# The first pair's turned keys in a PSUM tile per quarter, and idle products beside the first head's first scores

## The chip, the cores and the metric

The kernel runs on one core of one Trainium2 chip. The metric is the device time of one execution in microseconds (us), as the median of several runs. Engines are named as in the profile: PE is the matrix engine (TensorE) and PEld its weight loads, DVE is VectorE, ACT is ScalarE, POOL is GpSimd, SP is SyncE, which issues transfers; an engine's name with a q is its sequencer, which also issues transfers on ACT.

## The reference

An attention block with a threshold is followed by a feed-forward block with an ELU. Cut to what matters:

```python
# attention: q, k, v are (8, 8, 576, 64), float32; tau is a scalar
scores = scale * q @ k.T                        # scale = 1/8
thresh = max(scores, -1) - tau
scores = where(scores >= thresh, scores, -1e9)
attn = exp(scores - max(scores, -1))
out  = (attn / (sum(attn, -1) + 1e-9)) @ v      # to (4608, 512), heads side by side
# feed-forward: w_in (512, 2048), w_out (2048, 512)
h = x @ w_in
g = where(h > 0, h, exp(min(h, 0)) - 1)
result = g @ w_out
```

## The kernel before

Attention works on pairs of heads: 4 pairs in each of 8 sequences. A pair's two heads of 64 dimensions lie in the upper and the lower half of the 128 partitions, head 0 in rows 0 to 63 and head 1 in rows 64 to 127, so that a score product has 64 rows of the array. A step takes 128 query rows (the last, of 64 rows, serves both heads at once) against all 576 keys, in two halves of 288 (`HALF`); 512 of the 576 positions are `MAIN`, 64 are `TAIL`. A score product in float32 is two PE records in the trace. Feed-forward work of earlier sequences is laid among the attention steps later on. The order of all instructions is written out ahead: tasks have due times, corrected by a table (`MOVED`), are sorted, and each engine runs its own in that order, with semaphores between the engines. The first task is `start`; the scores of step 0 come after it.

For most pairs VectorE turns queries and keys in 32 by 32 squares. The first pair is turned by PE, in `start`:

- Transfers. SP's queue takes head 0's keys (`kb[:, 0]`, 128 KB), head 1's keys (`kb[:, 1]`), `tau`, and the second block of queries; ACT's queue takes the first block of queries (`qb[:, 0]`) and the last 64 keys of both heads (`ends`).
- Five PSUM tiles: `blank` and `turned` from the pool `t` (two buffers of one bank), `a`, `b`, `c` from the pool `s` (three buffers of two banks). `c` is taken and not used. The scores of step 0 get the buffers of `a` (head 0) and `b` (head 1).
- PE multiplies ones by ones twice (L1364), runs 8 transposes of the identity into `blank` (`warm`, whose records stand under L800), turns the queries (L1357), then two blocks of keys of head 0 into `a` and two of head 1 into `b`, runs one more idle transpose, and turns `ends`. A turn is one record with all 128 rows; `ends` uses 64.
- Copies out of PSUM into one SBUF tile that holds `qT` and `kT` (it shows as `x`): VectorE copies the queries (L1367); of each head's keys VectorE and ScalarE copy one half each, 64 rows by 256 columns (L1374), both out of the same tile; VectorE copies `ends` to their two places (L1377, and L1378 for head 1).
- `read_tau` then has five small GpSimd steps (L440 to L444) on tau, whose results the thresholds need.

`scores` (L665) issues the products of a step at L681. For the first two steps (`HEADS_APART`) both halves of head 0 stand ahead of both halves of head 1. Right after step 0's scores PE turns the second block of queries, and ScalarE copies it (`rest_of_first_q`, L1383); in ScalarE's order that copy stands ahead of all work on step 0's scores. For each head of step 0 VectorE then takes the maximum (`max_of`, L738) and a threshold (`pivot_of`, L756), ScalarE makes two passes (`sink_of`, L761, and `raise_of`, L767), VectorE adds up and inverts, and GpSimd scales (`normalize`, L734).

Of the kernel before, what the change touches and what calls it, by code (L numbers as in the profile page):

```python
# [368 lines left out]
def kernel(  # L369
# [10 lines left out]
    nc = tc.nc  # L380
    PSUM = bass.MemoryType.PSUM
    P = 128
    B, H, S, D = q.shape
    DM, DF = moe_w_in.shape
    NC = S // P
    MAIN = NC * P
    TAIL = S - MAIN
# [40 lines left out]
    ident = wstage.tile([P, P], FP32, name="ident", bufs=1)  # L428
# [10 lines left out]
    def read_tau():  # L439
        nc.gpsimd.tensor_scalar(keep, tau_sb, 0.0, SCALE, ALU.is_ge, ALU.mult)  # L440
        nc.gpsimd.tensor_scalar(far, keep, -FAR / SCALE, FAR, ALU.mult, ALU.add)
        nc.gpsimd.tensor_scalar(floor, tau_sb, far, 1.0, ALU.max, ALU.mult)
        nc.gpsimd.tensor_scalar(ntau, floor, DEEP, -1.0, ALU.min, ALU.mult)
        nc.gpsimd.tensor_scalar(ntau0, floor, -1.0 / SCALE, 1.0, ALU.mult, ALU.mult)  # L444
# [119 lines left out]
    def room_q(pr):  # L564
        if pr < 2:
            both = wstage.tile([P, 2 * S + TAIL], FP32, name="x", bufs=2)
            qT, firsts[pr] = both[:, :S], both[:, S:]
        else:
            qT = qkp.tile([P, S], FP32, name="qT")
        pairs[pr] = [qT, None, qds[pr % NQD]]  # L570
        return qT

    def room_k(pr):
        kT = pairs[pr][1] = firsts[pr] if pr < 2 else qkp.tile([P, TAIL + S], FP32, name="kT")
        return kT
# [19 lines left out]
    def long_rows(name, i):  # L595
        return {"k": k, "v": v}[name][0, i, :MAIN].rearrange("(p c) d -> p c d", c=NC)

    def first_rows(name, c, n=P):
        return {"q": q, "k": k}[name][0, :2, c * P : c * P + n].rearrange("i p d -> p i d")
# [56 lines left out]
    def vectors(pr):  # L656
        st = {x: small.tile([P, 2], FP32, name=x) for x in ("mx", "th", "su", "rs")}
        if not pr:
            st["nb"] = wstage.tile([P, 2], FP32, name="nb", bufs=4)
        step_no[0] += 1  # L660
        st["sm"] = totals[:, step_no[0] % 6]
        return st


    def scores(pr, i, hs):  # L665
        qT, kT, qd = pairs[pr]
        if hs[0] == 0:
            open_steps[pr, i] = vectors(pr)
        st = open_steps[pr, i]
        if "f" in psum and not apart:  # L670
            both = psum["s"].tile([P, 2, 2, 512], FP32, name="sc")
            scs = {h: both[:, h] for h in hs}
        else:
            scs = {h: psum["s"].tile([P, 2, 512], FP32, name="sc") for h in hs}
        halves = [(a, h) for a in range(2) for h in hs]
        if (pr, i) in HEADS_APART:
            halves.sort(key=lambda x: x[1])
        for a, h in halves:
            k0 = a * HALF + (0 if h else TAIL)
            r, qs = (slice(h * D, (h + 1) * D), qT[:, i * P : (i + 1) * P]) if i < NC else (slice(0, P), qd)  # L680
            nc.tensor.matmul(scs[h][:, a, :HALF], qs[r], kT[r, k0 : k0 + HALF], start=True, stop=True)  # L681
        if len(hs) == 2 and "f" in psum and not apart:
            st["both"] = both
        for h in hs:
            st[h] = scs[h]
# [113 lines left out]
    def transpose(dst, src):  # L799
        nc.tensor.matmul(dst, src, idents[-1], is_transpose=True, skip_group_check=True)  # L800
# [390 lines left out]
    def heads_of(i):  # L1191
        return [0, 1] if i < NC else [0]
# [123 lines left out]
    def early_tasks():  # L1316
# [18 lines left out]
        def start():  # L1335
            tiles = raws[0] = {"km": raw.tile([P, S // T, T], FP32, name="km")}
            kb = tiles["km"].rearrange("p j d -> p (j d)")[:, :MAIN].rearrange("p (i e f) -> p i e f", i=2, e=2)
            qb = wstage.tile([P, 2, 2, D], FP32, name="qb", bufs=1)
            ends = tiles["ends"] = wstage.tile([TAIL, 2, D], FP32, name="ends", bufs=1)

            nc.sync.dma_start(kb[:, 0], long_rows("k", 0).rearrange("p (e o) d -> p e (o d)", o=2))
            nc.scalar.dma_start(qb[:, 0], first_rows("q", 0))
            nc.sync.dma_start(kb[:, 1], long_rows("k", 1).rearrange("p (e o) d -> p e (o d)", o=2))
            nc.scalar.dma_start(ends, first_rows("k", NC, TAIL))
            nc.sync.dma_start(tau_sb, tau.to_broadcast([P, 1]))
            nc.sync.dma_start(qb[:, 1], first_rows("q", 1))
            nc.scalar.activation(keep, keep, AF.Exp)
            blank, turned = (psum["t"].tile([P, NC, P], FP32, name="rt", tag="rt") for _ in range(2))
            a, b, c = (psum["s"].tile([P, 2, 512], FP32, name="sc") for _ in range(3))
            qT, kT = room_q(0), room_k(0)  # L1350

            def warm(n):
                for _ in range(n):
                    transpose(blank[:, 0], ident)

            def turn_rows(dst, src, n=P):
                nc.tensor.matmul(dst, src, ident[:n, :n], is_transpose=True, skip_group_check=True)  # L1357

            def flat(src):
                return src.rearrange("p i d -> p (i d)")  # L1360

            ones = nc.const_aps.tensor(1.0, [P, P])
            for x in range(2):
                nc.tensor.matmul(blank[:, x], ones, ones, start=True, stop=True)  # L1364
            warm(8)
            turn_rows(turned[:, 0], flat(qb[:, 0]))
            nc.vector.tensor_copy(qT[:, :P], turned[:, 0])  # L1367
            main = kT[:, TAIL:S].rearrange("p (e o n) -> p o e n", e=2, o=2)
            for h, room in ((0, a), (1, b)):
                r = slice(h * D, (h + 1) * D)  # L1370
                for e in range(2):
                    turn_rows(room[:, 0, e * P : (e + 1) * P], kb[:, h, e])
                for o, copy in ((h, nc.vector.tensor_copy), (1 - h, nc.scalar.copy)):
                    copy(main[r, o], room[o * D : (o + 1) * D, 0, : 2 * P].rearrange("p (e n) -> p e n", e=2))  # L1374
            warm(1)
            turn_rows(turned[:, 1, :TAIL], flat(ends), TAIL)
            nc.vector.tensor_copy(kT[:, S:], turned[:, 1, :TAIL])  # L1377
            nc.vector.tensor_copy(kT[D:, :TAIL], turned[D:, 1, :TAIL])  # L1378

            def rest_of_first_q():  # L1380
                rt = psum["t"].tile([P, NC, P], FP32, name="rt", tag="rt")
                turn_rows(rt[:, 0], flat(qb[:, 1]))
                nc.scalar.copy(qT[:, P : 2 * P], rt[:, 0])  # L1383

            first_q.append(rest_of_first_q)
            read_tau()

# [16 lines left out]
        def switch():  # L1404
            first.close()
            apart.append(True)
            for name, bufs in (("s", 2), ("f", 2)):
                psum[name] = banks.enter_context(tc.tile_pool(name=f"ps_{name}", bufs=bufs, space=PSUM))

        task("start", -100.0, None, start)  # L1410
        for x in ("q", "k"):
            made["prep", x, 0] = made["copy", x, 0] = made["start"]
# [10 lines left out]
        for pr in range(1, NPAIR + 6):  # L1423
            old = ("sc", number[pr - 2, NC]) if pr > 1 else None
            own = pr < NPAIR
            for x, name in enumerate("qk"):
                n = 2 * pr - 2 + x if own else number[pr - 1, 2 + x]
                k, late_ = kind(n), n >= LATE
# [30 lines left out]
            for x, name in enumerate("qk"):  # L1459
                n = 2 * pr - 1 + x if own else number[pr - 1, 3 + x]  # L1460
# [3 lines left out]
            if pr > 1:  # L1464
                n = 2 * pr - 3 if own else number[pr - 1, 3]
# [5 lines left out]
        for i, (n, x) in enumerate(slots):  # L1471
            late_, k, t = n >= LATE, f"{kind(n)}{x}", begin[n]
# [42 lines left out]
        rooms, exps, owner = [], [], {}  # L1515
        for u in range(NU):
            n = 26 + 3 * u // 2 if u < NU - 2 else SWITCH + u - NU + 2
# [3 lines left out]
        for n in range(MIDDLE):  # L1521
            pr, i = steps[n]
# [4 lines left out]
            t, k, hs, late_ = begin[n], kind(n), heads_of(i), n >= LATE  # L1527
# [3 lines left out]
            if n == LATE:  # L1531
                task("switch", t, None, switch, *rooms)
            rooms += [("exp" if (n, h) in MASK_ACT else "mask", n, h) for h in hs]
            at_ = (lambda a, b, c=0: t + c) if last_ else (lambda a, b, c=0: t + b) if late_ else (lambda a, b, c=0: t + a)
            task(("sc", n), t + 0.2 if late_ else t - 2.6 if i in (2, NC) else t - 2.0, f"sc{k}", lambda pr=pr, i=i, hs=hs: (scores(pr, i, hs), first_q and first_q.pop()()), ("prep", "q", pr),
                 ("prep", "k", pr), ("scale", pr) if pr else None, ("copy", "k", pr), ("copy", "q", pr) if i == NC else None,
                 ("sc", n - 1) if n else None, "rest" if (pr, i) == (0, 2) else None, *two)
# [128 lines left out]
    with tc.manual_schedule():  # L1666
# [31 lines left out]
        ends = []  # L1698
# [439 lines left out]
        for pr in range(JOINED, NP + 2):  # L2138
            t = clock[0]
            b = pr // NPAIR  # L2140
# [265 lines left out]
```

## Time and profile before

| | us |
|---|---|
| median of three timed runs | 1256.07 |
| lowest and highest of them | 1256.03, 1256.32 |
| the profiled execution | 1257.65 |
| its span, first to last instruction | 1255.8 |
| PE busy in the span | 1244.7 (99%) |
| DVE, POOL, ACT busy | 1040.4, 727.8, 636.2 |

In the prediction a row of the timeline is: start, length (us from the span's start), engine, line of the kernel, operation, output<-input by the program's names, shape, xcount, and in brackets the idle time before it with what ended it. Rows that follow each other on one engine are merged and counted, and a short slice shows only what was under way in it. A row of the chain of waits is start, length and what; a row of transfers ends with its size and the time from issue to landing. The busy tenths on the page are 40 slices of 31.4 us each.

### The profile page before, as it was taken

The page shows a single profiled execution, that of the slowest core. Times are in us where ns is not written, and L with a number is a line of the kernel's source. Part 1 is how long each engine was busy: PE and PEld are TensorE (multiplying, and loading weights), DVE is VectorE, ACT ScalarE, POOL GpSimd, SP SyncE. Part 2 cuts the span into 40 slices and gives each one's busy share as a digit, 9 for nine tenths or more (in the row PEclk, how much of TensorE's full clock was granted, in tenths as well). Part 3 has the DMA queues.
Part 4 walks back from the last instruction along what each step waited for, and adds up shares of the span by engine and source line. Part 5 has one row for each costly group of instructions (what it writes and reads, how often), then busy time and mean ns, then how long its engine had stood idle before and what let it go on. Part 6 is the DMA issues. An engine that isn't in the chain of part 4 may idle for free.

```text
span 1255.8 us, 21112 instructions
## 1 busy us (share of the span) xinstructions
PE 1244.7 (99%) x6596; PEld 956.9 (76%) x6596; DVE 1040.4 (83%) x2196; ACT 636.2 (51%) x1334; POOL 727.8 (58%) x1064
## 2 busy tenths in 40 slices
PE   8999999999999999999999999999999999999998
PEld 6675576477887787878778787878788887788887
DVE  7888777789798978998889889898889876776983
ACT  7899776664453526253534445352625353465330
POOL 5778655687575748676576747584767655122000
PEclk9999999999999999999999999999999999999999
DMA  7456788998889998898989997999889885000001
GB/s 149 146 171 184 172 244 235 257 269 217 228 240 255 247 246 233 225 259 226 263 206 253 235 232 230 259 251 244 229 228 268 221 242 174 20 1 1 1 34 34
DMA packets 322303, 245.74 MB, mean 196 GB/s; under 512 B 205456, under 2 KB 286736, under 8 KB 322192
## 3 DMA queue, kind: packets, MB, share of 16 engines
q1 hardware_dynamic: 321376, 243.78, 72.3%
q8 instruction: 52, 0.85, 0.3%
q10 hardware_dynamic: 816, 0.62, 0.2%
q14 instruction: 59, 0.48, 0.2%
HBM read 154.53 MB, written 89.78 MB: 195 GB/s over the span
## 4 chain that ended last, share of the span: by engine, by line
PE 91%; DVE 3%; DMA 2%; ACT 2%; issue 1%; SPq 1%; POOL 1%; DVEq 0%; ACTq 0%; POOLq 0%
PE f L1869 23%; PE f L1729 21%; PE sc L985 8%; PE sc L1058 7%; PE f L2332 7%; PE f L2257 5%; PE f L1110 4%; PE sc L681 3%; PE f L1162 3%; PE f L2270 2%; PE pv L938 2%; PE rt L800 2%; PE sc L1050 1%; DMA there<-x 1%; PE sc L1045 1%
## 5 line engine op out<-in xcount | busy, mean ns | idle before, releaser
L992 DVE TENSOR_REDUCE mx<-sc 128x1 f32<-128x576 f32 x207 | 148.3, 750 | 30.0 <-PE sc L985 26.1
L734 POOL TENSOR_SCALAR w<-w,rs 128x576 f32<-128x576 f32 x144 | 115.8, 813 | 69.6 <-DVE rs L797 69.5
L1012 ACT ACTIVATE w<-sc,mx 128x576 f32<-128x576 f32 x113 | 81.5, 740 | 115.6 <-DVE mx L992 98.7
L876 DVE STREAM_TRANSPOSE x<-w 128x512 f32<-128x512 f32 (+1 forms) x153 | 108.9, 744 | 12.9 <-POOL w L734 11.5
L1004 POOL TENSOR_SCALAR th<-mx,ntau 128x2 f32<-128x2 f32 (+1 forms) x114 | 33.8, 296 | 134.5 <-DVE mx L992 134.5
L985 PE MATMUL sc<-kT,qT 64*128 64x448 f32 (+4 forms) x736 | 103.1, 416 | 0.2 <-ACT xs L1074 0.2
L985 PEld LDWEIGHTS sc<-kT,qT 64*128 64x128 f32 x736 | 80.7, 186 | 25.2 <-issue 16.2
L1019 DVE SCALAR_TENSOR_TENSOR w<-sc,th,w 128x576 f32<-128x576 f32 x113 | 88.2, 810 | 9.4 <-ACT w L1012 9.2
L1729 PE MATMUL f<-xt,sw 128*128 128x256 f32 x384 | 93.4, 386 | 0.4 <-DVE g L1751 0.4
L1729 PE MATMUL f<-xt,w_in 128*128 128x256 f32 x384 | 92.3, 382 | 0.0
L1869 PE MATMUL f<-w_out,s 128*128 128x256 f32 x384 | 92.0, 382 | 0.1
L1869 PE MATMUL f<-w_out,g 128*128 128x256 f32 x384 | 92.0, 382 | 0.0
L1729 PE MATMUL f<-x,w_in 128*128 128x256 f32 x384 | 90.9, 379 | 0.1
L1869 PE MATMUL f<-t,s 128*128 128x256 f32 x384 | 90.8, 379 | 0.0
L734 POOL TENSOR_SCALAR e<-e,rs 128x576 f32<-128x576 f32 x91 | 67.1, 741 | 35.3 <-DVE rs L797 33.9
L1729 PEld LDWEIGHTS f<-xt,sw 128*128 128x128 f32 x384 | 69.5, 189 | 16.7 <-issue 5.4
L1729 PEld LDWEIGHTS f<-xt,w_in 128*128 128x128 f32 x384 | 71.7, 190 | 12.8 <-ACT w L1743 2.2
L1869 PEld LDWEIGHTS f<-w_out,g 128*128 128x128 f32 x384 | 72.0, 190 | 12.4 <-issue 3.1
L1869 PEld LDWEIGHTS f<-w_out,s 128*128 128x128 f32 x384 | 71.9, 190 | 12.4 <-issue 2.5
L1729 PEld LDWEIGHTS f<-x,w_in 128*128 128x128 f32 x384 | 72.8, 190 | 10.5 <-ACT s L1743 0.7
L1869 PEld LDWEIGHTS f<-t,s 128*128 128x128 f32 x384 | 72.8, 190 | 10.3 <-POOL s L1816 0.4
L1816 POOL TENSOR_TENSOR s<-g 128x256 f32<-128x256 f32 x96 | 74.9, 785 | 8.0 <-DVE g L1779 7.5
(330 smaller groups left out, 3106.3 us busy)
## 6 DMA issues: line engine op xcount, KB each, us to landing
there<-x SPq DMA_DIRECT2D x444, 144.0 KB, 3.5
wTb<-there SPq DMA_DIRECT2D x58, 576.0 KB, 6.4
wTa<-there SPq DMA_DIRECT2D x53, 576.0 KB, 4.8
sw<-win_sums SPq DMA_DIRECT2D x46, 384.0 KB, 4.5
t<-wout_sums SPq DMA_DIRECT2D x33, 512.0 KB, 6.2
qm<-in_q_dram SPq DMA_DIRECT2D x124, 72.0 KB, 4.9
wst<-in_moe_w_in_dram SPq DMA_DIRECT2D x16, 512.0 KB, 4.5
vm<-in_v_dram SPq DMA_DIRECT2D x64, 128.0 KB, 3.8
```

The costliest lines, as they stand in the source:

```text
L734: nc.gpsimd.tensor_scalar(wv, wv, st["rs"][:, h : h + 1], 1.0, ALU.mult, ALU.mult)
L876: nc.vector.transpose(x[:, :, c0 : c0 + nc_], src.rearrange("p (c g n) -> p g c n", c=nc_, n=T))
L985: on_banks(nc.tensor.matmul(o, qT[r, i * P : (i + 1) * P], kT[r, k0 : k0 + n], start=True, stop=True, skip_group_check=True), o)
L992: on_banks(nc.vector.tensor_reduce(st["mx"][:, h : h + 1], st["sc", h], axis=AX.XY if i == NC else AX.X, op=ALU.max, negate=True), st["sc" ...
L1012: on_banks(nc.scalar.activation(st["e", h], st["sc", h], AF.Exp, bias=st["mx"][:, h : h + 1]), st["sc", h])
L1019: on_banks(nc.vector.scalar_tensor_tensor(st["e", h], st["sc", h], st["th"][:, h : h + 1], st["e", h], ALU.is_ge, ALU.mult, accum_out=st[" ...
L1058: on_banks(nc.tensor.matmul(o, vm[:, h, c], parts[part][:, g0:g1, h * (NC + 1) + c], start=False, stop=(c == NC - 1), skip_group_check=Tru ...
L1729: nc.tensor.matmul(loc["banks"][place], left[:, j], right[:, j], start=(begins and j == 0), stop=(j == 1), skip_group_check=True)
L1816: engine.tensor_tensor(o, x, y, op)
L1869: nc.tensor.matmul(place(m), lhs, rhs, start=(begins and v == 0), stop=(v == RU - 1), skip_group_check=True)
L2257: nc.tensor.matmul(o, w.rearrange("p (j f) -> p j f", j=KJ)[:, j], m, start=(j == 0 and x == 0), stop=(j == KJ - 1 and x == 1), skip_group ...
L2332: nc.tensor.matmul(banks8[2 * i + x // 2], h[:, tok], w, start=(f == 0 and x != 1), stop=(f == NFT - 1 and x != 0), skip_group_check=True)
```

## The change

It does three things in `start` and one in `scores`.

1. Each quarter of the first pair's turned keys gets a tile of its own: head 0's two blocks go to `a` and `b`, head 1's to `c` and the second quarter of `blank`. A block is copied by one engine, VectorE for the first and ScalarE for the second of each head, in two copies of 64 rows by 128 columns.
2. The order of turns: 6 idle transposes instead of 8, then head 0's keys, the queries, one idle transpose, head 1's keys, `ends`. On VectorE the queries' copy stands behind head 0's keys.
3. The second transfer of the two queues is swapped: `ends` on SP's, head 1's keys on ACT's.
4. After each of head 0's two score products of step 0, two products of the lower half of the identity by itself (64 rows, 128 columns, float32) are issued on rows 64 to 127; they write to the second bank of `b`, which head 1's second half overwrites.

```diff
+    beside = []
...
             nc.tensor.matmul(scs[h][:, a, :HALF], qs[r], kT[r, k0 : k0 + HALF], start=True, stop=True)
+            if (pr, i, h) == (0, 0, 0):
+                beside[0]()
...
-            nc.sync.dma_start(kb[:, 1], long_rows("k", 1).rearrange("p (e o) d -> p e (o d)", o=2))
-            nc.scalar.dma_start(ends, first_rows("k", NC, TAIL))
+            nc.sync.dma_start(ends, first_rows("k", NC, TAIL))
+            nc.scalar.dma_start(kb[:, 1], long_rows("k", 1).rearrange("p (e o) d -> p e (o d)", o=2))
...
-            warm(8)
+            def turn_keys(h, rooms):
+                for e in range(2):
+                    turn_rows(rooms[e], kb[:, h, e])
+
+            def copy_keys(h, rooms):
+                for e, copy in ((0, nc.vector.tensor_copy), (1, nc.scalar.copy)):
+                    for o in range(2):
+                        k0 = TAIL + (2 * e + o) * P
+                        copy(kT[h * D : (h + 1) * D, k0 : k0 + P], rooms[e][o * D : (o + 1) * D])
+
+            warm(6)
+            sides = (a[:, 0, :P], b[:, 0, :P]), (c[:, 0, :P], blank[:, 1])
+            turn_keys(0, sides[0])
             turn_rows(turned[:, 0], flat(qb[:, 0]))
+            copy_keys(0, sides[0])
             nc.vector.tensor_copy(qT[:, :P], turned[:, 0])
-            main = kT[:, TAIL:S].rearrange("p (e o n) -> p o e n", e=2, o=2)
-            for h, room in ((0, a), (1, b)):
-                r = slice(h * D, (h + 1) * D)
-                for e in range(2):
-                    turn_rows(room[:, 0, e * P : (e + 1) * P], kb[:, h, e])
-                for o, copy in ((h, nc.vector.tensor_copy), (1 - h, nc.scalar.copy)):
-                    copy(main[r, o], room[o * D : (o + 1) * D, 0, : 2 * P].rearrange("p (e n) -> p e n", e=2))
             warm(1)
+            turn_keys(1, sides[1])
             turn_rows(turned[:, 1, :TAIL], flat(ends), TAIL)
+            copy_keys(1, sides[1])
             nc.vector.tensor_copy(kT[:, S:], turned[:, 1, :TAIL])
...
+            def beside_one_head():
+                for x in range(2):
+                    nc.tensor.matmul(b[:, 1, x * P : (x + 1) * P], ident[D:], ident[D:], start=True, stop=True)
+
+            beside.append(beside_one_head)
```

## The prediction

> **What bounds the kernel now.** I read the page first, then the chain of waits over the first 14 us, then the timeline of the same stretch, and last the timeline in slices short enough to single out the first score products.
>
> ```profile
> span 1255.8 us, 21112 instructions
> ...
> PE   8999999999999999999999999999999999999998
> ...
> PE 91%; DVE 3%; DMA 2%; ACT 2%; issue 1%; SPq 1%; POOL 1%; DVEq 0%; ACTq 0%; POOLq 0%
> ```
>
> The matrix engine carries 91% of the chain, and the only slice short of full besides the last is the first. The change touches only the first 8 us of that slice, so it can shift the start of everything and nothing else. The chain there (start, length, what):
>
> ```profile
> 5.23 1.38 PE sc L681 x4
> ...
> 6.64 0.77 DVE mx L738
> ...
> 7.51 0.27 DVE th L756
> 7.78 0.67 DVE mx L738
> ...
> 8.48 0.28 DVE th L756
> ...
> 9.52 0.29 ACT w L767
> ...
> 10.19 0.96 ACT w L767 x3
> ...
> 11.70 1.33 POOL w L734 x2
> ...
> 13.95 1.25 PE sc L681 x5
> ```
>
> After the warming products and turns come the first scores (5.2), the maximum of head 0, its threshold, the maximum of head 1, its threshold, the ScalarE work on both heads until 11.15, the GpSimd scaling, and the scores at 13.95. No transfer is on it. What moves the ScalarE stretch moves all that follows.
>
> **Part 1: the turned keys, by quarters.**
>
> ```profile
> 1.74 1.92 PE L800 MATMUL rt<-ident 128*128 128x128 f32 x8
> ...
> 3.32 0.18 PEld L1357 LDWEIGHTS rt<-ident,qb 128*128 128x128 f32 x1
> 3.45 0.42 PE L1357 MATMUL rt<-ident,qb 128*128 128x128 f32 x1
> ...
> 3.66 1.06 PE L1357 MATMUL sc<-ident,km 128*128 128x128 f32 x4
> 3.91 0.29 DVE L1367 COPY x<-rt 128x128 f32<-128x128 f32 x1 [2.93 <-PE rt L1357]
> ...
> 4.33 0.88 DVE L1374 COPY x<-sc 64x256 f32<-64x256 f32 x2
> 4.52 0.42 PE L800 MATMUL rt<-ident 128*128 128x128 f32 x1
> 4.79 0.82 ACT L1374 COPY x<-sc 64x256 f32<-64x256 f32 x2 [1.30 <-DVE x L1374]
> ...
> 4.87 0.37 PE L1357 MATMUL rt<-ident,ends 64*128 64x64 f32 x1
> ...
> 5.27 0.23 DVE L1377 COPY x<-rt 128x64 f32<-128x64 f32 x1
> ...
> 5.53 0.23 DVE L1378 COPY x<-rt 64x64 f32<-64x64 f32 x1
> ...
> 7.41 0.27 ACT L1383 COPY x<-rt 128x128 f32<-128x128 f32 x1 [1.80 <-PE rt L1357]
> ```
>
> ```profile
> km<-in_k_dram SPq DMA_DIRECT2D x2, 128.0 KB, 2.4
> ...
> ends<-in_k_dram ACTq DMA_DIRECT2D x1, 32.0 KB, 3.3
> ```
>
> The ScalarE copy stood 1.30 us idle until VectorE's copy of the same tile was over, though the two read different rows: one PSUM tile is read by one engine at a time. That wait goes, since every tile now has one reader.
>
> Turns. They step by 0.21 (1.06 for four, the last 0.42 long). Six warming products from 1.74 leave the engine free at 3.02. The first key block is issued at 0.72 and lands about 2.35 later, at 3.05; with 0.13 from weight load to product (3.32 to 3.45) the two turns of head 0 start at 3.20 and 3.41, the query turn at 3.62 (3.45 before), the warming one at 3.84, head 1's at 4.05 and 4.26, the ends at 4.61 (the step from 128 rows to 64 took 4.52 to 4.87).
>
> VectorE. A result is there 0.42 + 0.04 after its turn starts. A copy of 128 columns I price at 0.29 on VectorE and 0.27 on ScalarE (L1367, L1383; half the rows, same columns), 0.03 apart. Head 0: 3.66 to 4.27; queries 4.30 to 4.59; head 1: 4.62 to 5.23; ends 5.26 to 5.49 and 5.52 to 5.75 (5.50 and 5.76 before). Each engine now has four copies, 1.16 on VectorE where two took 0.88, so VectorE becomes the bound and the second copy of the ends, which head 1 needs, comes no earlier. ScalarE does head 0 by 4.43 and head 1 by 5.3 (5.61 before), hidden behind VectorE.
>
> Transfers. The second key block moves to ScalarE's queue, issued 1.23 instead of 1.17: it lands near 3.7, needed at 4.05, hidden. The ends, at 1.17 on SyncE's queue, land by 4.5, needed at 4.61; lateness there costs one for one only past 5.0, as VectorE reads that turn at 5.26. Behind them tau and the second query block slip by at most 0.3:
>
> ```profile
> 1.17 0.42 SPq L1343 DMA_DIRECT2D km<-in_k_dram  x1
> ...
> 1.23 0.73 ACTq L1344 DMA_DIRECT2D ends<-in_k_dram  x1
> ...
> 5.03 0.23 POOL L440 TENSOR_SCALAR keep<-tau_sb 128x1 f32<-128x1 f32 x1 [2.93 <-DMA tau_sb<-in_tau_dram]
> ...
> 6.32 0.19 POOL L444 TENSOR_SCALAR ntau<-floor 128x1 f32<-128x1 f32 x1
> ```
>
> (0.73 less 0.42 of issue). GpSimd's chain from tau would end at 6.8, needed by the threshold at 7.2; the query block is needed near 7.2 too and lands by 5.5. Both are free.
>
> Scores of head 0. Queries at 4.59 + 0.05, matrix engine free at 4.61 + 0.11: first product at 4.72, 0.49 sooner.
>
> ```profile
> 5.21 0.67 PE L681 MATMUL sc<-x 64*128 64x288 f32 x1
> ...
> 5.71 0.40 PE L681 MATMUL sc<-x 64*128 64x288 f32 x1
> ...
> 5.90 0.48 PE L681 MATMUL sc<-x 64*128 64x288 f32 x2
> ...
> 6.46 0.64 PE L681 MATMUL sc<-x 64*128 64x288 f32 x2
> ...
> 6.64 0.76 DVE L738 TENSOR_REDUCE mx<-sc 128x1 f32<-128x576 f32 x1 [0.88 <-PE sc L681]
> ...
> 9.87 1.97 PE L800 MATMUL rt<-ident 128*128 128x128 f32 x16
> ```
>
> The array runs at half rate at first: eight transposes in 1.92 us at 1.74, sixteen in 1.97 at 9.87. The change of rate falls near 5.6: the product from 5.21 took 0.50 to the next one, the last two, 6.46 and 6.70 (7.10 less 0.40), step by 0.24. (The page's granted clock does not show it.) If 5.6 holds, head 0's four records (two to a product) start at 4.72, 5.22, 5.66, 5.90, the last 0.40 long; the maximum starts at 6.34 instead of 6.64. So of 0.49 some 0.30 is left: more of the work falls into the slow stretch.
>
> **Part 2: the idle products.** Four products of 128 columns, two records each: eight records, on rows 64 to 127, ahead of head 1's scores. No row shows such a record; at full rate the transposes' 0.11 apiece bounds it below, at half rate 0.21 above. Below nothing they could only be worth if they brought the rate up sooner, and no row shows that. Beside head 0's own records they cost head 0 nothing if the two row halves run at once. Before, they did: 5.90 is 0.19 after 5.71, closer than two records of one half (0.24), and head 0's four must be 5.21, 5.71, 5.95 and 6.19, the last ending at 6.6, to let the maximum start at 6.64; so head 1's first ran before head 0's third, which stands ahead of it in the program. I take eight records from 4.82, at 0.21 until 5.6 and 0.11 after: done at 6.07. Head 1 starts there instead of 5.90.
>
> ```profile
> 7.04 0.33 PE L1357 MATMUL rt<-ident,qb 128*128 128x128 f32 x1
> ...
> 7.70 0.75 DVE L738 TENSOR_REDUCE mx<-sc 128x1 f32<-128x576 f32 x1
> ...
> 7.82 1.80 ACT L761 ACTIVATE w<-sc,th,keep 128x576 f32<-128x576 f32 x2
> ```
>
> Its last record is at 6.87, the turn of the second query block at 7.20 (6.70 to 7.04 before), its ScalarE copy from 7.57 to 7.84. That copy stands in front of head 0's first ScalarE pass (L761), which had 0.15 us to spare; now it decides: 7.87 instead of 7.82, though the threshold is ready at 7.5. Head 1's maximum starts at 7.40 (7.70), its threshold ends at 8.46; the second pass starts at the later of 8.50 and 7.87 + 0.73 (9.52 less 8.79, the step of back-to-back passes) = 8.60, against 8.79 before (9.62 less 0.83). **Sum: 0.19 us off the ScalarE stretch**, which runs without a break to the totals after 11.15. Late next is ScalarE itself, not the scores. Ends of the one uncertain term, head 1's start: 5.90 gives 0.29 off; 6.45 (next part) makes it 0.2 later.
>
> [...]
>
> The profiled execution took 1257.65 us, 1.85 beyond its span of 1255.8; the three timed runs have a median of 1256.07. I put the 0.19 to the median: 1255.9.
>
> **Rivals.**
> 1. *The gain is lost on the way.* 0.2 us at 11 us must survive to the end. For it: other engines have slack, and waits between 14 and 60 us change hands often. Against: the chain there has no transfer that starts by itself. Time 1256.0 to 1256.2.
> 2. *More is gained*, because head 1 is not held up or a wait farther on falls differently: 1255.2 to 1255.6.
> 3. *Slower: the records start in program order.* Then the second four idle records come after head 0's fourth at 5.90, and run to about 6.45; head 1's last is at 7.25, the query copy from 7.95 to 8.22, the passes at 8.25 and 8.98, 0.19 late: 1256.3. It decides once head 1 starts after 6.25 (from there 8.79 cannot be held).
> [...]
> 5. *The change does nothing*: the copies still wait on each other, and head 1 stays the bound: 1256.1, with rival 1.
>
> **How the numbers follow.** Forecast 0.55 (1255.7 to 1256.0); rivals 1 and 5 together 0.18; rival 2 0.09; rival 3 0.11; rival 4 0.07. The forecast's 0.55, rivals 1, 5 and most of 2 and 3 lie in 1255.2 to 1256.6, which leaves out rival 4 and tails. 0.2% is 2.5 us, about what a measurement of this kernel can tell from no change; the whole start before the first scores is 5.2 us, and nothing priced here reaches half of 2.5 but the extreme of rival 4. So: same 0.94, slower 0.04, faster 0.02.
>
> **What would show it.** The first ScalarE key copy should start near 3.9, not 4.79, with no wait on VectorE; the first score product near 4.7; the maximum of head 0 near 6.3; head 1's maximum near 7.4; the query copy near 7.6 directly before the first pass at 7.9; the second pass near 8.6; the totals at 11.0 and the scores now at 13.95 near 13.75. [...] A changed order of steps after 14 us, or a shift there that is not the one at 11 us, would make the forecast wrong.

## The result, and the profile after

| | before | after |
|---|---|---|
| median (lowest to highest), 19 runs each, us | 1256.21 (1255.85 to 1258.34) | 1258.83 (1256.97 to 1260.10) |
| ratio of the comparable runs | | 1.0017, 95% from 1.001 to 1.0024 |
| the profiled execution; its span, us | 1257.65; 1255.8 | 1259.29; 1257.5 |

The kernel became slower: 2.6 us by the medians, 0.17% by the ratio. The forecast of 1255.9 and its range up to 1256.6 do not hold it. The ratio leaves out 1, so the loss is clear of the noise. The 19 times of after fall into two groups, six from 1256.97 to 1257.48 and thirteen from 1258.57 up; the profiled execution is of the second, and the experiments bear on what parts them.

The page of after has the same shares in its chain of waits, within 1%, and shows nothing of the loss:

```profile
span 1257.5 us, 21127 instructions
...
PE 91%; DVE 3%; ACT 2%; DMA 1%; issue 1%; POOL 1%; SPq 1%; DVEq 0%; ACTq 0%; POOLq 0%
```

The timeline of after in its first 12 us (columns as before; the new lines are L1377 for the key copies, L1399 for the idle products, L1395 for the query copy, L683 scores, L742 maximum, L765 first ScalarE pass, L795 totals):

```profile
3.76 0.55 ACT L1377 COPY x<-sc 64x128 f32<-64x128 f32 x2 [0.52 <-PE sc L1361]
...
4.52 0.58 PE L1399 MATMUL sc<-ident 64*128 64x128 f32 x1
4.67 0.79 PE L683 MATMUL sc<-x 64*128 64x288 f32 x1
4.89 0.63 PE L1399 MATMUL sc<-ident 64*128 64x128 f32 x2
5.26 0.68 PE L683 MATMUL sc<-x 64*128 64x288 f32 x1
5.32 0.65 PE L1399 MATMUL sc<-ident 64*128 64x128 f32 x2
5.74 0.68 PE L683 MATMUL sc<-x 64*128 64x288 f32 x1
5.77 0.84 PE L1399 MATMUL sc<-ident 64*128 64x128 f32 x3
6.22 1.41 PE L683 MATMUL sc<-x 64*128 64x288 f32 x5
...
6.84 0.76 DVE L742 TENSOR_REDUCE mx<-sc 128x1 f32<-128x576 f32 x1 [1.25 <-PE sc L683]
7.92 0.27 ACT L1395 COPY x<-rt 128x128 f32<-128x128 f32 x1 [2.79 <-PE rt L1361]
8.09 1.74 ACT L765 ACTIVATE w<-sc,th,keep 128x576 f32<-128x576 f32 x2
11.37 0.16 DVE L795 TENSOR_REDUCE su<-sm 128x2 f32<-128x4 f32 x1
```

The start does what was said of it, but at half the rate for longer: ScalarE's copies wait for PE alone, the first score product stands at 4.67, and the idle records lie beside head 0's. Head 0's records still step by 0.48 to 0.59 up to 6.22, so the maximum is at 6.84, and the totals are at 11.37, 0.20 later than before's 11.17. That is less than a tenth of the loss. The rest is in the chain of waits 15 us later, in step 4 (the first step of the third pair). Its VectorE line is: two masks with their sums (`mask_of`, L783, now L787), totals, reciprocal, and the scaling of one head (`normalize_dve`, L717, now L721), which PE's transposes wait for. Before:

```profile
26.09 0.83 DVE w L783 x3
...
27.34 0.53 DVE w L717
...
28.01 0.63 PE rt L800 x4
...
29.07 1.88 PE pv L938 x16
30.95 0.59 PE rt L800 x4
```

After:

```profile
26.28 0.08 DVE w L787
26.37 0.20 issue
26.57 0.84 DVE w L787 x2
...
27.83 1.53 DVE w L721
...
29.49 0.63 PE rt L804 x4
...
30.55 3.54 PE pv L942 x16
34.09 0.59 PE rt L804 x4
```

Three things add to the 0.2 of the start. (1) Before the second mask VectorE stands 0.20 us idle, with "issue" as the cause, which in the profile means that it waited for nothing that is shown; in before the mask started at once, beside the 0.08 in which the first mask's sum is read out. The mask is 0.28 later by that, and the delay is now 0.48. (2) The scaling takes 1.53 instead of 0.53, and PE resumes 1.48 late. (3) Sixteen products (L942) take 3.54 instead of 1.88, and the transposes after them stand 3.14 late (34.09 against 30.95). PE's wait for the scaling, in before and then in after (who waits for whom: us in total, times, longest):

```profile
PE rt L800 <- DVE w L717: 0.3, 1, 0.3
```

```profile
PE rt L804 <- DVE w L721: 1.6, 1, 1.6
```

For (2), the timeline of GpSimd beside the scaling has `convert_add`, an integer addition on feed-forward weights. Before:

```profile
27.34 0.52 DVE L717 TENSOR_SCALAR w<-w,rs 128x576 f32<-128x576 f32 x1
27.55 1.47 POOL L502 TENSOR_TENSOR wtop<-wtop,wst 128x512 int32<-128x512 int32 x1 [1.11 <-ACT wst L487]
```

After:

```profile
27.74 1.27 POOL L502 TENSOR_TENSOR wtop<-wtop,wst 128x512 int32<-128x512 int32 x1 [1.12 <-ACT wst L487]
27.83 1.52 DVE L721 TENSOR_SCALAR w<-w,rs 128x576 f32<-128x576 f32 x1
```

The scaling stood 0.20 us ahead of the addition; now it starts 0.08 behind it, with 1.18 of the addition still to come (27.74 and 1.27, to 29.01), and is 1.00 longer. GpSimd's addition moved with the start, by 0.20; the scaling moved with the start and the mask's pause, by 0.48. A lead of 0.20 was lost to a pause of 0.28.

For (3), the page's 40 slices are too coarse; short windows show the granted clock in after and then in before (the stretch and its length; busy time and instructions of PE, PEld, DVE, ACT and POOL; the granted clock, where 1.00 is the full rate; the share of DMA, and GB/s):

```profile
30.50:33.80 3.30, 3.30 (x17) 1.69 (x16) 3.23 (x9) 2.84 (x5) 0.50 (x2) 0.50 0.93 240
```

```profile
30.50:33.80 3.30, 3.30 (x29) 2.27 (x24) 2.87 (x9) 2.60 (x7) 1.45 (x3) 1.00 0.92 223
```

A microsecond after the pause the array went to half rate. The clock events kept in the trace put it from 30.478 to 33.891, 3.413 us.

The spans differ by only 1.7, not 3.1, because the profiled execution of before had a wait of its own. In its chain of waits PE stands for a transfer:

```profile
549.73 6.61 DMA there<-x
...
556.36 7.87 DMA wTb<-there
```

where the chain of after has only feed-forward products:

```profile
553.62 12.37 PE f L1746 x56
```

That wait took 1.4 of the shift back. Against before's median of 1256.21 the profiled 1259.29 is 3.08 late, which is close to the 3.14 of step 4.

### The profile page after: what moved, and what is told of

It reads as the page before. It is cut to its first block, busy times and chain, and to the rows that moved or that the text cites. A ratio compares the mean times of both kernels' runs of the same rounds, so it can differ in the third digit from the quotient of the medians.

```text
span 1257.5 us, 21127 instructions
## 1 busy us (share of the span) xinstructions
PE 1245.9 (99%) x6602; PEld 958.2 (76%) x6602; DVE 1041.4 (83%) x2198; ACT 635.9 (51%) x1336; POOL 727.9 (58%) x1064
## 4 chain that ended last, share of the span: by engine, by line
PE 91%; DVE 3%; ACT 2%; DMA 1%; issue 1%; POOL 1%; SPq 1%; DVEq 0%; ACTq 0%; POOLq 0%
PE f L1746 23%; PE f L1886 22%; PE sc L989 8%; PE sc L1062 7%; PE f L2349 7%; PE f L2274 5%; PE f L1114 4%; PE sc L683 3%; PE f L1166 3%; PE f L2287 2%; PE pv L942 2%; PE rt L804 2%; PE sc L1054 1%; PE sc L1049 1%; DVE x L880 1%
```

## The experiments

Theory A, after the result: the scaling falls behind the addition, and PE's longer pause brings the rate down. Theory B, in its several forms: something else costs the time, such as the idle products, or any later start by itself. Theory C came after the first four runs and says why the scaling falls behind: the two copies that the change adds on VectorE move the second mask of step 4 from the place of VectorE's 62nd instruction in the trace (semaphore instructions counted) to that of the 64th, and there it pauses. Its rival D: the quarters delay the mask in another way. In each run the shift can be read at one place, the start of the transposes behind the sixteen products (30.95 in before). "Before" beside the experiments is 1256.24 (29 runs) for the first four, 1256.23 (28) for the next four, 1256.76 (23) for the last two.

**The quarters without the idle products.**

```diff
-            if (pr, i, h) == (0, 0, 0):
-                beside[0]()
```

> The changed kernel without the idle products; the quarters, the order of turns and the swapped transfers stay. Theory A (the cost arises near 28 us: VectorE's scaling of step 4 comes 0.08 us behind GpSimd's long add, stands behind it for about 1.0 us, and the pause on PE that follows lets the array's rate fall for 3.4 us): head 0's scores come earlier, the race near 28 us has another outcome only if VectorE gains over 0.1 us on GpSimd; if it still loses, about 1257.1 without the fall of rate and 1258.9 with it. Theory B (the idle products themselves, in the slow first scores, cost the time): 1256.0 or a little less, with the same pause at 28 us gone for no other reason.

1259.30 (1258.20 to 1261.64), ratio 1.0024 (1.0013 to 1.0035). The waits of PE near step 4, and the mask:

```profile
PE rt L802 <- DVE w L719: 1.6, 1, 1.6
```

```profile
28.10 0.82 DVE L785 SCALAR_TENSOR_TENSOR w<-sc,th,e 128x576 f32<-128x576 f32 x1 [0.21 <-issue]
```

The loss is there without idle products, so they are not needed for it. The profiled 1259.20 is made up otherwise: the rate rose only at 13.06, the first mask of step 4 was at 27.05, 1.70 later than before's 25.35, and the rate did not fall after the pause (granted clock 1.00 from 30.60 to 33.00).

**The idle products without the quarters** (before, with `beside_one_head` called as in the change).

> The kernel before with the idle products alone. Theory A: head 1's scores later by up to 0.3 us, the stretch at 28 us decides: 1256.1 to 1256.4 if VectorE is still ahead of GpSimd there, about 1257.1 or 1258.9 if not. Theory B: as the changed kernel, 1258.8.

1256.63 (1256.45 to 1260.27), ratio 1.0006 (0.9997 to 1.0015). VectorE has no new instruction here: the mask starts at once, the scaling at 27.71 takes 0.52 ahead of the addition at 27.92, PE waits 0.3. The totals are at 11.55, 0.38 late: in the old order of turns the first score product is 0.16 later (5.37 against 5.21), and the idle records run until head 1's first record starts at 6.82, where before's stands at 5.90. The median is above the 1256.1 to 1256.4 that was expected, but the interval of the ratio takes in 1, so the times do not show a cost. One of the eleven took 1260.27; there is no trace of that one.

**The addition later**: the changed kernel with a one-column GpSimd copy ahead of the addition.

```diff
+            if i == 1:
+                nc.gpsimd.tensor_copy(far, staged[i][:, :, 0].bitcast(FP32)[:, :1])
```

> The changed kernel with one small GpSimd copy (one column, about 0.2 us, waiting for the same ScalarE step) put in front of GpSimd's second weight add, the one near 27.7 us. Theory A: VectorE's scaling (L721 of the changed kernel) is ahead again and takes 0.5 us instead of 1.5, the pause on PE after 27.9 us shrinks from 1.57 to about 0.5 us, the rate does not fall at 30.5 us, and the median comes back to 1256.2 to 1256.6. Theory B: no change, 1258.8.

1259.07 (1257.05 to 1260.41), ratio 1.0017 (1.0008 to 1.0026): a miss. The copy was too short:

```profile
27.77 1.28 POOL L504 TENSOR_TENSOR wtop<-wtop,wst 128x512 int32<-128x512 int32 x1
27.80 1.58 DVE L723 TENSOR_SCALAR w<-w,rs 128x576 f32<-128x576 f32 x1
```

The addition was still first, by 0.02, and the scaling took 1.58. It did not test what it was made for; it shows how little decides.

**The pause filled**: ten idle transposes of PE in step 4 of the changed kernel.

```diff
-IDLES = {(2, 2, 2), (5, 0, 9), (6, 1, 3), (7, 0, 1), (7, 1, 1)}
+IDLES = {(2, 2, 2), (4, 0, 10), (5, 0, 9), (6, 1, 3), (7, 0, 1), (7, 1, 1)}
```

> The changed kernel with ten idle transposes (1.1 us at full rate) in the pause on PE after 27.9 us. Theory A: VectorE still stands behind GpSimd (1.5 us), but the rate does not fall at about 30 us: all runs near 1257.1, none near 1258.9. Theory B: no change, 1258.8, since the pause is not the cause.

1257.78 (1257.04 to 1258.45), ratio 1.001 (1.0001 to 1.0019). Its window, and its totals:

```profile
30.50:33.80 3.30, 3.30 (x29) 2.00 (x25) 2.99 (x8) 3.30 (x6) 0.51 (x3) 1.00 0.98 236
```

```profile
11.02 0.16 DVE L795 TENSOR_REDUCE su<-sm 128x2 f32<-128x4 f32 x1
```

No fall of the rate, and all of its eleven times lie below after's upper group. This points to the two groups of after as runs with and without the fall, which cost 1.66 in the profile. The mean granted clock of the runs agrees (0.998 in nine of the thirteen upper runs, 0.999 or more in all six lower ones), but no trace of a lower run is there to show it. Not all came down to 1257.1 as expected: six of the eleven lie between 1257.78 and 1258.45, and why is not shown. The mask's pause (0.21) and the late scaling (1.55) are still there. In this profile the rate rose at 5.63, the moment that the prediction assumed, and the totals are at 11.02, 0.15 sooner than before's 11.17, where 0.19 was forecast.

**The order turned round in before**: two more small sums on VectorE ahead of step 4's totals.

```diff
+            if (pr, i) == late_step:
+                for _ in range(2):
+                    nc.vector.tensor_reduce(st["su"][:, cs], st["sm"][:, cs], axis=AX.X, op=ALU.add)
```

> The kernel before with two more small VectorE sums (0.19 us each) in front of the totals of step 4, whose result they repeat. Theory A (the order of VectorE's scaling and GpSimd's add near 27.5 us decides): VectorE comes 0.2 us behind, stands for about 1.0 us, and the time rises to 1257.1 to 1258.8. If the order does not matter: 1256.5, the 0.38 us alone.

1258.99 (1257.11 to 1260.79), ratio 1.0016 (1.0007 to 1.0025). The mask starts at once, but:

```profile
29.32 1.28 POOL L502 TENSOR_TENSOR wtop<-wtop,wst 128x512 int32<-128x512 int32 x1 [1.12 <-ACT wst L487]
29.49 1.43 DVE L717 TENSOR_SCALAR w<-w,rs 128x576 f32<-128x576 f32 x1
```

A delay of 0.4 us at this place alone, in the kernel before, turns the order round and gives a loss like that of the change, the rate's fall included (from 30.56). The profiled 1260.72 also holds a late rise of the rate, at 13.49, with the order of turns of before.

**A later start of before**: ten warming transposes instead of eight.

```diff
-            warm(8)
+            warm(10)
```

> The kernel before with ten warming transposes instead of eight: everything from the first turn on 0.43 us later. Theory A and C: VectorE and GpSimd shift together, the scaling stays ahead, 1256.4 to 1256.7. Theory B (a later start by itself upsets the stretch at 28 us): 1257 to 1259.

1256.68 (1256.36 to 1258.36), ratio 1.0003 (0.9994 to 1.0012). Scaling ahead, at 27.28 for 0.52; PE waits 0.3. But the totals stand at 11.12, no later than before, since the rate rose sooner (3.92): it does not test a later start. The last but one experiment does.

**The mask moved off the 64th place**: the changed kernel, VectorE's first memset cut in nine, eight more instructions of VectorE at a time when it has nothing to do.

```diff
-    nc.vector.memset(qds[0], 0.0)
+    for x in range(9):
+        nc.vector.memset(qds[0][:, x * 8 : x * 8 + 8 if x < 8 else P], 0.0)
```

> The changed kernel with VectorE's first clearing of a tile cut into nine pieces: eight more VectorE instructions before 2 us, where VectorE is idle until 3.5 us; nothing else moves. In the three kernels with the quarters profiled beside the changed one, the second mask of step 4 (L787) started 0.2 us late with nothing to wait for, and it is the 64th VectorE row in each; in the two without the quarters it is the 62nd and starts at once. Theory C (a pause at that place in VectorE's list of instructions, which the two added copies moved onto the mask): the mask starts at once, VectorE's scaling is ahead of GpSimd's add again (0.5 us, not 1.5), the pause on PE near 28 us is 0.3 us, and the median is 1255.9 to 1256.3, at or under the kernel before. Rival D (the quarters' other effects, as tiles or semaphores, delay the mask): no change, 1258.8.

1255.85 (1255.72 to 1256.61), ratio 0.9995 (0.9986 to 1.0003).

```profile
26.38 0.82 DVE L788 SCALAR_TENSOR_TENSOR w<-sc,th,e 128x576 f32<-128x576 f32 x1
27.63 0.52 DVE L722 TENSOR_SCALAR w<-w,rs 128x576 f32<-128x576 f32 x1
27.84 1.46 POOL L503 TENSOR_TENSOR wtop<-wtop,wst 128x512 int32<-128x512 int32 x1 [1.12 <-ACT wst L488]
```

```profile
PE rt L805 <- DVE w L722: 0.3, 1, 0.3
```

No pause of the mask, the old order, PE's old wait, no fall (granted clock 1.00 from 30.60 to 33.00): the whole loss is gone, with the change's turns, copies and idle products untouched. The profiled execution is the slowest of the eleven (1256.61); in it the rate rose at 6.59 and the totals are at 11.45.

**The mask moved onto the 64th place in before**: its memset cut in three, two more instructions, nothing of the change.

> The kernel before with the same clearing cut into three: two more VectorE instructions before 2 us and nothing else. Theory C: the second mask of step 4 becomes the 64th row, starts 0.2 to 0.3 us late, VectorE's scaling falls behind GpSimd's add (1.5 us), PE pauses 1.6 us near 28 us, and the median rises to 1257.1 where the array's rate holds and 1258.8 where it falls: the whole loss without any of the change. Rival D: 1256.2.

1260.11 (1259.07 to 1261.55), ratio 1.0029 (1.0017 to 1.004). Its mask, and the sixteen products in its chain:

```profile
26.35 0.82 DVE L784 SCALAR_TENSOR_TENSOR w<-sc,th,e 128x576 f32<-128x576 f32 x1 [0.21 <-issue]
```

```profile
27.60 1.53 DVE w L718
...
31.17 2.66 PE pv L939 x16
33.83 0.59 PE rt L801 x4
```

The whole loss without any part of the change. The median is higher still than after's; the profiled execution is the fastest of the six, so what the others had on top is not shown.

**The quarters without idle products, mask moved off** (the first and the seventh edit together).

> The quarters alone (no idle products), with VectorE's first memset cut in nine so that step 4's second mask no longer is VectorE's 64th row. If the loss is the pause at that row and the changed order of scaling and addition that follows: the mask starts at once, the scaling takes 0.52 us ahead of GpSimd's addition, PE pauses 0.28 and not 1.58, and the time falls from the 1259.3 of the quarters alone to between 1255.9 and 1257.5. The place in that range tells what the idle products are worth: 1255.9, as with them, if they do nothing; 1256.8 to 1257.5, with the array's rate rising after 10 us as in the profile of the quarters alone, if they bring the rise forward. If the quarters cost something by themselves later on: 1258.5 or more.

1258.01, but in two groups: five of twelve from 1255.93 to 1256.89, seven from 1258.00 to 1258.98; ratio 1.0002 (0.9994 to 1.0011). The profiled run is of the second group (1258.25): the scores of step 0 and, in its waits of PE near step 4,

```profile
4.78 3.32 PE L684 MATMUL sc<-x 64*128 64x288 f32 x8
...
12.90 0.15 DVE L794 TENSOR_REDUCE su<-sm 128x2 f32<-128x4 f32 x1
```

```profile
PE rt L803 <- DVE w L720: 0.3, 1, 0.3
```

The totals are 1.73 late, the rate rose at 12.95, and yet the scaling stays ahead of the addition (29.07 and 29.27): a later start alone does not turn the order round. The median lies above the expected 1255.9 to 1257.5, because of the second group. With the idle products, in the kernel of the seventh experiment, no run of eleven lay above 1256.61; without them eight of twelve did. But the two were not measured together, and of before's own runs beside them 9 of 28 and then 12 of 23 lay above 1256.61, so these times alone do not give the worth of the idle products.

**Before with the memset cut in nine**, the control for both.

> The kernel before with its memset cut in nine and nothing else: the control for the same cut in the changed kernel. If the cut only moves which instruction is the 64th row: 1256.2, as before, scaling ahead of the addition, PE pause 0.28; then the 0.38 us by which the changed kernel with the cut stands under before belong to the change. If the cut itself saves time elsewhere: 1255.8. If eight small instructions cost something: up to 1256.8 (they would delay the start by at most 0.5).

1256.21 (1255.84 to 1258.99), ratio 0.9996 (0.9987 to 1.0004). The eight score records take 1.90 us, totals at 11.07, scaling ahead: the cut does nothing by itself that can be measured.

**All profiles at one place.** Start of the transposes behind the sixteen products of step 4, the time of the same execution, and the time less the start:

| kernel | start, us | time, us | difference |
|---|---|---|---|
| after | 34.09 | 1259.29 | 1225.20 |
| quarters alone | 33.95 | 1259.20 | 1225.25 |
| idle products alone | 31.31 | 1256.62 | 1225.31 |
| addition later | 34.09 | 1259.31 | 1225.22 |
| pause filled | 32.06 | 1257.34 | 1225.28 |
| before, sums in step 4 | 35.37 | 1260.72 | 1225.35 |
| before, ten warming | 30.88 | 1256.65 | 1225.77 |
| after, mask off 64th | 31.23 | 1256.61 | 1225.38 |
| before, mask on 64th | 33.83 | 1259.07 | 1225.24 |
| quarters, mask off 64th | 32.67 | 1258.25 | 1225.58 |
| before, memset in nine | 30.87 | 1256.21 | 1225.34 |
| before (transfer wait at 564) | 30.95 | 1257.65 | 1226.70 |

From there on nine of twelve take 1225.2 to 1225.4, and two more are within 0.4 of that: what a kernel lost or gained in the first 35 us it kept to the end.

## Why the prediction was wrong, point by point

- **The step that failed** is in the first part: "it can shift the start of everything and nothing else". The change also adds instructions: two copies on VectorE, where it has time to spare, moved the mask from its 62nd instruction to its 64th, where it waited 0.20. None of the rivals had this mechanism. The runs showed in place of that step: 0.28 us at the mask, 1.00 for the order of scaling and addition, and 1.66 for the rate. The prediction named a shift after 14 us that is not the one at 11 us as what would make it wrong, and that is what came. It did not look at how close the next meeting of two engines was, though before's timeline shows it: 0.20 us between scaling and addition.
- **A shift is carried to the end**: right, and more strictly than argued, by the table. No profile shows rival 1, a gain lost on the way.
- **The copies**: right. ScalarE's first key copy at 3.76 (forecast near 3.9), without a wait on VectorE; first score product at 4.67 (4.72). (The landing at 3.05 is a slip, as 0.72 and 2.35 make 3.07; the 3.20 that follows is right.)
- **The path through the query copy**: right. ScalarE's copy at 7.92 stands directly ahead of the first pass at 8.09, though the pass came 0.17 after the start of the copy, where 0.30 was taken.
- **The row halves at once**: right. All eight idle records start before head 0's fourth at 6.22, and the first, at 4.52, before head 0's first at 4.67; by program order (rival 3) four of them would have come after head 0's fourth.
- **"If 5.6 holds"**: mis-sized. The 5.6 was read rightly from the widths (the clock events of before's trace have 5.57), but in the profile of after the rate rose at 6.59, with head 0's maximum at 6.84 instead of 6.34 and the totals at 11.37 instead of 10.98. A rise later still costs more: at 12.95, in the profile of the quarters with the mask moved off, the totals are 1.73 late. Over twelve profiles the moment lies between 3.9 and 6.6 in nine and between 12.9 and 13.5 in three (PE records between 10 and 12 us: 16 to 18 in the nine, 8 in the three). No run shows what sets the moment, nor the term behind the chance of 0.07 for a late rise (rival 4); the runs showed only when the rate rose.
- **The sum, 0.19 us**: borne out in the one profile where the rate rises as assumed (0.15 with the pause filled). In the times it is only suggested: with the mask moved off, 1255.85 against 1256.23 is a gain of 0.38, but the interval of the ratio takes in 1, and the profile of that kernel, with the late 6.59, has the totals 0.28 later than before's.
- **Bounding the idle products below**: it said that only a sooner rise of the rate could make them a gain, "and no row shows that". The profiles suggest it now and do not settle it: the rate rose by 6.6 in all five with idle products, and of the seven without, by 6.6 in four and between 12.9 and 13.5 in three; the kernels are not otherwise alike. In the old order of turns the idle products cost 0.38 at the totals.
- **The chance for slower**, 0.04, followed from the same first step: "nothing priced here reaches half of 2.5 but the extreme of rival 4". The result stands at the edge of that 0.2%: 2.6 us by the medians, 0.17% by the ratio.

What is left open: why the mask pauses. It did so, for 0.20 to 0.21 us, in all five kernels in which the second mask was VectorE's 64th instruction, and in none of the seven in which it was the 62nd, 70th or 72nd; in before another instruction, the totals, has that place and does not pause.

## What to carry to other kernels

When an edit adds or removes instructions on an engine, even early and in idle time, look through the later timeline for meetings with little to spare (here VectorE's scaling beside GpSimd's addition, 0.20 us, lost to a delay of 0.28), and price what turns round if one of them slips. To tell such a loss from the edit's own worth, add a few instructions that do nothing of weight on that engine, to the kernel before and to the one after: here two of them made the whole loss and eight took it away. Compare several profiles at one fixed instruction behind the edit: this parts what an edit did from what the run did.

## What the runs showed of the hardware that was not expected

- VectorE's scaling of 128x576 took 0.52 us when it started ahead of GpSimd's addition and 1.43 to 1.58 when it started 0.02 to 0.17 behind it. In after it took 1.00 longer than in before, with 1.18 of the addition left when it started; what makes it longer is not shown.
- In a PE pause of about 1.6 us, or up to 1.0 us behind it, the array went to half rate in four kernels: in the changed one for 3.41 us (30.478 to 33.891), in the same with the addition later, and in two that differ from before only on VectorE (memset in three, sums in step 4); the granted clock of each was 0.50 from 30.60 to 32.70. With the pause filled PE waited 0.4 and the clock was 1.00. It was not so in every run: the quarters alone had the pause (1.58, from 29.43 to 31.01) and a clock of 1.00 from 30.60 to 32.70. So the length of the pause alone does not tell whether the rate falls. By the clock events the fall came 23.893 after the first rise in after (6.585 to 30.478), seven times 3.413, and 17.07 after it with the sums in step 4 (13.49 to 30.56), five times. An estimate from these: counted on in the same length from its rise at 13.06, a fall in the quarters alone could have come at 30.13, in the middle of the pause, with 0.70 of it ahead; ahead of the falls there lay 1.57 of the pause in after and 1.07 with the sums. Whether this is what kept the rate up is not shown.
- The rise of the rate at the start comes between 3.9 and 13.5 us for work that differs little, and the totals of step 0, or the first mask of step 4, are then 1.7 to 1.8 us later (12.90 against 11.17; 27.12 and 27.05 against 25.35).
